# A list scheduler in the kernel file sets the order of a fused attention and feed-forward kernel

## The chip, the cores and the metric

The kernel runs on one core of one Trainium2 chip. The metric is the device time of one execution in microseconds, and of several runs the median. Names of engines: PE (TensorE matmuls) with PEld (its weight loads), DVE (VectorE), ACT (ScalarE), POOL (GpSimd, here only issuing stores), SP (SyncE, issuing loads and the output's stores).

## What is computed

Channel attention over q, k, v of 4 x 6080 x 256, whose result of 24320 rows of 256 goes through a feed-forward layer of width 2048 with a squared ReLU:

```python
qn = q / (np.linalg.norm(q, axis=1, keepdims=True) + 1e-06)
kn = k / (np.linalg.norm(k, axis=1, keepdims=True) + 1e-06)
s = kn.transpose(0, 2, 1) @ qn / tau
s = s - s.max(-1, keepdims=True)
a = np.exp(s)
a /= a.sum(-1, keepdims=True) + 1e-09
x = v @ a
...
h = x @ w_in
r = np.maximum(h, 0.0)
g = r * r
return g @ w_out
```

The attention matrix a is only 256 x 256 for each of the 4 batches.

## The kernel before

**Precision.** Every f32 operand of a large matmul is split into a high half (a cast to fp32r) and a low half (f32 minus the high half, again fp32r), and a product is three matmuls: high by high, low by high, high by low. So each operand costs a cast (on ACT in the kernel before) and a subtraction (on DVE).

**Work per batch.** The scores k'q are summed over 48 tiles of 128 rows, two at a time (`score_load`, `score_norm`, `score_split`, `score_mm`, `score_add`). Batch 0, and the first 24 tiles of batch 1 (the early scores, EARLY = 12 pairs), go through plain f32 matmuls on x and on an output bank (L175), the rest through split ones. `norms`, `spread`, `exps` and `attnT` make the softmax and turn it round. `fold` multiplies w_in by the attention matrix (L294), so that v is multiplied by the folded weights alone; `combine` makes from them the seven weight combinations of a Strassen product, wt, which POOL stores to memory (wsc, L320) and SP loads again for each later chunk (`load_wt`, L333; three buffers).

**Work per quad.** A batch's 6080 rows are 6 chunks of 2 x 512 (the last 2 x 480) rows; for each chunk there are 8 tiles j of the hidden width, and a pair (chunk, j) is a quad: 192 in all. The first layer of a quad is seven products, `m1` to `m7`, of three matmuls each, all issued on L386 in `product`. Their banks in PSUM are h (two), x and z:

- `m1` writes h; ACT copies it to x (L437). `m6` adds to h; ACT copies that to z (L445). `m4` adds to h again.
- `m7` writes the other h; ACT copies it to the tile m (L460).
- `m2` adds to x; ACT takes its ReLU to r (L452). `m5` adds to z, and DVE adds m to z with a ReLU, into s (L465); only then may `m3` add to z again; ACT takes the ReLU of that to r (L487). DVE also adds m to the h of `m4` (L465).
- `pair` squares s or r on ACT (L397), casts it to the high half of g (L401; on DVE, L399, for the last three j of a chunk and r alone) and subtracts (DVE, L402).

The second layer (`layer2`, `layer2s`, `run_later`, all on L547 in `accumulate`) multiplies g by w_out into four output banks o and, in chunks 2 to 23, j = 0, 2 and 4, saves products by a second Strassen scheme (`combos`, `split_later`; tiles D and t).

**What sets the order.** The program emits steps in the order of a plan (per quad `m1, m7, 0, m6, m2, 1, m5, m4, 2, m3`, where the numbers stand for second-layer products of the quad before). Side work (scores, folds, loads, splits of v) is put at fractional places between quads with `at`; `tie` adds an ordering edge, so that an instruction of side work doesn't come earlier than AHEAD = 1.0 quads before its place on PE, ACT and DVE. The framework's scheduler then orders everything by priority; copies out of PSUM are raised:

```python
459         with tc.high_priority():
460             nc.scalar.copy(out=state[q]["m7"][:, :T], in_=H[:, :T])
```

At the start six matmuls on a tile of ones run while the first loads are under way:

```python
635     busy = h_bank()
636     for _ in range(6):
637         nc.tensor.matmul(out=busy[:, :P], lhsT=ones, rhs=ones, start=True, stop=True)
```

Each engine executes its own instructions strictly in the order in which they stand, waiting on semaphores of the others.

## Time and profile before

| | |
|---|---|
| median of 3 runs | 2157.55 us (2156.49 to 2157.71) |
| the profiled execution, its own time | 2155.96 us |
| span of its instructions | 2154.2 us, 27293 instructions |
| PE / PEld busy | 2133.3 us (99%) / 1757.4 us (82%) |
| DVE / ACT busy | 1648.3 us (77%) / 1657.7 us (77%) |
| POOL busy | 42.7 us (2%) |
| DMA | 452.55 MB, mean 210 GB/s |

The busy time of PE is the union of its matmuls' times. Matmuls are pipelined and their ends are modelled: the mean duration of one is 389 ns where they follow each other every 226 ns or so, and a matmul that waits a little for its weights shows no idle time. An f32 matmul on unsplit tiles appears as two passes. The execution's own time has 1.8 us more than the span of its instructions.

### The profile page before, as it was taken

Reading aid. Unit: us, or ns where it says so; the run is one execution under the profiler, and the core shown is the slowest. Engines: PE = TensorE matmul, PEld = TensorE weight load, DVE = VectorE, ACT = ScalarE, POOL = GpSimd, SP = SyncE. Lnnn points to the kernel's source line nnn. Section 1 sums busy time; section 2 is a strip of 40 time slices with the busy share of each in tenths; the row PEclk is TensorE's granted clock in tenths of the full one; section 3 lists DMA queues with packets and bytes.
Section 4 is the critical chain, followed back from the end, with each engine's and each line's share of the span. In section 5 each row is a group of like instructions: output and inputs, shape, how many; then the busy total and the mean of one; then the engine's idle time right before and its main releaser. Section 6 shows DMA issues by size and latency. Waiting matters only on the chain.

```text
span 2154.2 us, 27293 instructions
## 1 busy us (share of the span) xinstructions
PE 2133.3 (99%) x9710; PEld 1757.4 (82%) x9710; DVE 1648.3 (77%) x2336; ACT 1657.7 (77%) x2512; POOL 42.7 (2%) x69
## 2 busy tenths in 40 slices
PE   9999999999999999999999999999999999999999
PEld 8778888878888888887888888888788788787787
DVE  6887778868779888786787978878778667667666
ACT  6788787877878878788788788877877767767766
POOL 0111000000000000000000000000000000000000
PEclk9999999999999999999999999999999999999999
DMA  9758755457585574556667656555566555555552
GB/s 351 290 228 310 249 174 212 157 206 249 194 288 206 176 247 166 197 180 210 232 214 256 230 176 223 177 194 194 201 234 226 197 189 181 181 184 186 181 169 90
DMA packets 125224, 452.55 MB, mean 210 GB/s; under 512 B 12928, under 2 KB 33920, under 8 KB 125088
## 3 DMA queue, kind: packets, MB, share of 16 engines
q1 hardware_dynamic: 117792, 412.40, 55.3%
q0 software_dynamic: 7296, 38.41, 4.5%
q8 instruction: 77, 1.26, 0.2%
q14 instruction: 59, 0.48, 0.1%
HBM read 387.45 MB, written 63.31 MB: 209 GB/s over the span
## 4 chain that ended last, share of the span: by engine, by line
PE 87%; ACT 7%; DVE 5%; issue 1%; DMA 1%; SPq 0%; ACTq 0%; DVEq 0%
PE o L547 34%; PE h L386 21%; PE z L386 11%; PE h L547 8%; PE x L386 5%; PE h L175 4%; PE h L294 2%; PE x L175 2%; DVE g L402 1%; DVE s L465 1%; ACT s L397 1%; ACT r L397 1%; ACT g L401 1%; ACT m L460 1%; ACT r L487 1%
## 5 line engine op out<-in xcount | busy, mean ns | idle before, releaser
L547 PE MATMUL o<-g,wo 128*128 128x512 f32 (+1 forms) x3420 | 896.2, 389 | 0.6 <-ACT g L401 0.4
L547 PEld LDWEIGHTS o<-g,wo 128*128 128x128 f32 x3420 | 637.3, 188 | 137.4 <-DVE g L402 8.9
L386 PE MATMUL h<-vt,wt 128*128 128x512 f32 (+1 forms) x2304 | 630.7, 389 | 4.1 <-ACT m L460 2.9
L386 PEld LDWEIGHTS h<-vt,wt 128*128 128x128 f32 x2304 | 430.5, 188 | 98.7 <-ACT m L460 5.6
L386 PE MATMUL z<-vt,wt 128*128 128x512 f32 (+1 forms) x1152 | 332.9, 393 | 4.0 <-ACT z L445 2.6
L402 DVE TENSOR_TENSOR g<-s,g 128x1024 fp32r<-128x1024 f32 (+1 forms) x126 | 152.8, 1213 | 174.4 <-ACT g L401 174.3
L402 DVE TENSOR_TENSOR g<-r,g 128x1024 fp32r<-128x1024 f32 (+1 forms) x192 | 232.5, 1211 | 52.3 <-ACT g L401 49.9
L386 PEld LDWEIGHTS z<-vt,wt 128*128 128x128 f32 x1152 | 209.2, 188 | 55.8 <-DVE s L465 12.5
L397 ACT ACTIVATE s<-s 128x1024 f32<-128x1024 f32 (+1 forms) x126 | 132.7, 1053 | 134.3 <-DVE s L465 134.0
L397 ACT ACTIVATE r<-r 128x1024 f32<-128x1024 f32 (+1 forms) x192 | 202.7, 1056 | 1.1
L386 PE MATMUL x<-vt,wt 128*128 128x512 f32 (+1 forms) x576 | 161.7, 387 | 0.0
L437 ACT COPY x<-h 128x512 f32<-128x512 f32 (+1 forms) x192 | 111.0, 578 | 49.3 <-PE h L386 47.4
L422 ACT ACTIVATE D<-D 128x1024 f32<-128x1024 f32 (+1 forms) x66 | 69.4, 1052 | 98.7 <-DVE D L465 98.4
L487 ACT ACTIVATE r<-z 128x512 f32<-128x512 f32 (+1 forms) x192 | 112.3, 585 | 42.8 <-PE z L386 41.7
L401 ACT CAST g<-s 128x1024 fp32r<-128x1024 f32 (+1 forms) x126 | 131.6, 1045 | 0.7
L386 PEld LDWEIGHTS x<-vt,wt 128*128 128x128 f32 x576 | 108.1, 188 | 21.8
L401 ACT CAST g<-r 128x1024 fp32r<-128x1024 f32 (+1 forms) x120 | 124.9, 1040 | 0.0
L155 DVE TENSOR_TENSOR acc<-acc,sq 128x1024 f32<-128x1024 f32 x92 | 112.1, 1219 | 11.8 <-ACT sq L154 9.4
L452 ACT ACTIVATE r<-x 128x512 f32<-128x512 f32 (+1 forms) x192 | 114.2, 595 | 4.2 <-DVE g L402 1.7
L445 ACT COPY z<-h 128x512 f32<-128x512 f32 (+1 forms) x192 | 112.6, 587 | 5.6 <-PE h L386 4.8
L460 ACT COPY m<-h 128x512 f32<-128x512 f32 (+1 forms) x192 | 111.6, 581 | 4.8 <-PE h L386 4.2
L373 DVE TENSOR_TENSOR vt<-v,vt 128x512 fp32r<-128x512 f32 (+1 forms) x144 | 94.2, 681 | 25.8 <-ACT vt L372 25.8
(154 smaller groups left out, 2726.1 us busy)
## 6 DMA issues: line engine op xcount, KB each, us to landing
wt<-wsc SPq DMA_DIRECT2D x184, 896.0 KB, 4.9
wo<-wop SPq DMA_DIRECT2D x118, 512.0 KB, 3.6
kq<-kq SPq DMA_DIRECT2D x87, 512.0 KB, 5.3
wo<-wodM SPq DMA_DIRECT2D x88, 384.0 KB, 4.2
wsc<-wt POOLq DMA_DIRECT2D x32, 896.0 KB, 5.8
wo<-wos SPq DMA_DIRECT2D x66, 384.0 KB, 3.6
v<-vT SPq DMA_DIRECT2D x40, 512.0 KB, 7.1
outT<-uM SPq DMA_DIRECT2D x80, 256.0 KB, 3.4
```

Source lines behind the costliest of these rows:

```text
L155: nc.vector.tensor_add(out=accs[b], in0=accs[b], in1=sq)
L175: nc.tensor.matmul(out=s[:, h * C:(h + 1) * C], lhsT=l, rhs=r, start=first and h == 0 and n == 0, stop=last and n == len(terms) - 1, skip_ ...
L386: nc.tensor.matmul(out=out[:, :T], lhsT=w[:, l, i], rhs=v[:, r, :T], start=start and n == 0, stop=n == 2, skip_group_check=True)
L397: nc.scalar.activation(out=x, in_=x, func=AF.Square)
L401: nc.scalar.copy(out=h, in_=x)
L402: nc.vector.tensor_sub(out=l, in0=x, in1=h)
L437: nc.scalar.copy(out=st["X"][:, :T], in_=st["B"][:, :T])
L445: nc.scalar.copy(out=st["Z"][:, :T], in_=st["B"][:, :T])
L452: nc.scalar.activation(out=state[q]["r"][:, 0, :T], in_=state[q]["X"][:, :T], func=AF.Relu)
L460: nc.scalar.copy(out=state[q]["m7"][:, :T], in_=H[:, :T])
L487: nc.scalar.activation(out=r[:, 1, :T], in_=state[q]["Z"][:, :T], func=AF.Relu)
L547: nc.tensor.matmul(out=o[:, :T], lhsT=l, rhs=r[:, :T], start=start and k == 0, stop=stop and k == 2)
```

## The change

The whole body is rewritten into two steps. First every operation is recorded with `add`: a key (its place in quads, as `at` had it), the engines that may do it with a cost for each, the tiles that it reads and writes, and a function that emits it. Then `Plan.order` runs a list scheduler over all operations, from front to back in its own time: for each of PE, ACT, DVE, SP and POOL it takes, whenever that engine is free, one of the operations whose inputs are ready and whose buffers are free. PE, SP and POOL take the one with the lowest key within a window (0.7 quads for PE); ACT and DVE take the one whose result is due first, counted back from PE's order, where DVE treats an operation that either engine could do as due 3.0 us later. The costs are lines in the number of columns (`vec`, `vec1`, `act`, `mm3`) and fixed latencies. What comes out is emitted with the framework's own ordering switched off (`tc.manual_schedule()`); the framework still places the semaphores and buffers.

Casts to fp32r (`split`) may now go to either engine; the copies out of PSUM (`moved`) stay on ACT, sums and subtractions on DVE. The products, their number and their tiling, the number of loads and stores and the sizes of the buffers stay. The six matmuls on ones are gone. Of the 24 early score tiles of batch 1, the last six (from LEAD = 18 on) get keys within the first quad. On PE the new program has 9534 matmul instructions where the old has 9540; on DVE there are 408 casts to fp32r where there were 72, on ACT 332 instructions fewer.

```diff
+    LAT = {"P": 0.22, "A": 0.16, "V": 0.14}
...
+    def __init__(self, rings, ahead, loose):
+        self.rings = rings
+        self.loose = loose
+        self.shy = {"V": 3.0}
+        self.ahead = ahead
...
+    def add(self, key, engines, fn, r=(), w=(), size=0):
...
+            if t in self.writer:
+                op.deps.add(self.writer[t])
...
+    def order(self):
...
+                    for op in waiting[e]:
+                        if op.ready > now + 1e-9 or op.key > place + self.ahead[e]:
+                            continue
+                        rank = (op.key, op.n) if e in "PSG" else (
+                            op.due + self.shy.get(e, 0.0) * (len(op.engines) > 1), op.n)
+                        if best is not None and rank >= best[0]:
+                            continue
+                        need = {}
+                        for name in op.tiles:
+                            if name not in live:
+                                need.setdefault(self.ring_of[name], []).append(turn[name])
+                        if any(free[ring] < len(n) or ring not in self.loose and max(n) >= served[ring] + len(n)
+                               for ring, n in need.items()):
+                            continue
+                        best = rank, op
+                    if best is None:
+                        continue
...
+                    op.begun = now
+                    out.append((op, e))
+                    at[e] = now + op.engines[e]
+                    done = at[e] + self.LAT.get(e, 0.0)
...
+def vec(n):
+    return 0.07 + 0.00104 * n
+
+
+def vec1(n):
+    return 0.07 + 0.00052 * n
+
+
+def act(n):
+    return 0.1 + 0.00083 * n
...
+    LEAD = 18
...
+    RINGS = {"kq": 4, "g2": 3, "D": 3, "hl": 2, "t4": 1, "s": 2, "sq": 2, "wo": 6, "wt": 3, "vt": 8, "v": 1, "tt": 1,
+             "m7": 2, "uM1": 1, "uM5": 1, "uM6": 1, "uM7": 1, "acc": 1, "s_acc": 1, "zq": 1, "e": 2, "den": 2,
+             "aT": 1, "y": 3, "nm": 2,
+             "h": 2, "x": 1, "z": 1, "o00": 1, "o01": 1, "o10": 1, "o11": 1}
+    plan = Plan(RINGS, {"P": 0.7, "A": 1.2, "V": 1.2, "S": 2.0, "G": 2.0}, ("h",))
...
+    def cast(n):
+        return {"A": act(n), "V": vec1(n)}
+
+    def alu(key, n, fn, r, w):
+        add(key, {"V": vec(n)}, lambda e: fn(), r, w)
+
+    def split(key, n, x, h, l, r, wh, wl):
+        add(key, cast(n), lambda e: copy(e, h(), x()), r, wh)
+        add(key, {"V": vec(n)}, lambda e: nc.vector.tensor_sub(out=l(), in0=x(), in1=h()), (*r, *wh), wl)
...
-    def pair(q, x, cs):
-        T = chunks[q[0]][2]
-        hl = work.tile([P, 2, 2, HMAX], F32R, name="g2", tag="g2", bufs=GB)
-        h, l = hl[:, 0, :, :T], hl[:, 1, :, :T]
-        nc.scalar.activation(out=x, in_=x, func=AF.Square)
-        if cs[0] == "11" and q[1] >= NJ - 3:
-            nc.vector.tensor_copy(out=h, in_=x)
-        else:
-            nc.scalar.copy(out=h, in_=x)
...
+    def pair(key, q, s, cs, view):
+        T = chunks[q[0]][2]
+        g = plan.tile("g2", ("g", q, cs))
+        add(key, {"A": act(2 * T)}, lambda e: square(e, view(), view()), [(s, 0), (s, 1)],
+            [(s, 0), (s, 1)])
+        split(key, 2 * T, view, lambda: get(g, [P, 2, 2, HMAX], F32R)[:, 0, :, :T],
+              lambda: get(g, [P, 2, 2, HMAX], F32R)[:, 1, :, :T], [(s, 0), (s, 1)], [(g, 0)], [(g, 1)])
...
-    def m7(q):
-        T = chunks[q[0]][2]
-        H = h_bank()
-        product(q, S3, H, True)
-        state[q]["m7"] = work.tile([P, HMAX], F32, name="m7")
-        with tc.high_priority():
-            nc.scalar.copy(out=state[q]["m7"][:, :T], in_=H[:, :T])
...
+    def m7(key, q):
+        T = chunks[q[0]][2]
+        H, m = plan.tile("h", ("H", q)), plan.tile("m7", ("m7", q))
+        product(key, q, S3, H, True)
+        add(key, moved(T), lambda e: copy(e, get(m, [P, HMAX])[:, :T], made[H][:, :T]), [(H, 0)], [(m, 0)])
...
-    busy = h_bank()
-    for _ in range(6):
-        nc.tensor.matmul(out=busy[:, :P], lhsT=ones, rhs=ones, start=True, stop=True)
...
+            at(-0.6 + 0.01 * k if k < LEAD else 0.02 + 0.9 * (k - LEAD) / (2 * EARLY - LEAD),
+               lambda key, g=g, t=t, k=k: score_mm(key, tiles0[1, g], t, s1, k == 0, k == EARLY * G - 1))
...
-    def tie(u, fn, args):
-        behind = next((last for t, last in reversed(marks) if t <= u - AHEAD), {})
-        n0 = len(traced())
-        fn(*args)
-        for ins in traced()[n0:]:
-            if ins.engine in behind:
-                tc.add_manual_dep(ins, behind[ins.engine],
-                                  mybir.DependencyInfo(mybir.DependencyClass.NoSync, mybir.DependencyReason.DATA),
-                                  reason="side work keeps its place")
...
+    for u, _, fn, args in sorted(events, key=lambda x: x[:2]):
+        fn(u, *args)
+    with tc.manual_schedule():
+        for op, e in plan.order():
+            op.fn(e)
```

Three places, each before and now. Ahead of a row's number of repetitions stand the tiles (out<-in) and the size.

PE from the end of the first pair of folds to the first second-layer products. L175 (L418 in the changed file) are the early scores on an output bank, L294 (L552) the folds, L386 (L661) the seven products, L547 (L805) the second layer. Before:

```order
L294 MATMUL h<-hl,aTl 128x512
L175 MATMUL o_369<-kq 128x256 x12
L175 MATMUL o_369<-g_337 128x256 x4
L175 MATMUL o_369<-g_367 128x256 x4
L175 MATMUL o_369<-D 128x256 x12
L386 MATMUL h<-vt,wt 128x512 x9
L386 MATMUL x<-vt,wt 128x512 x3
L386 MATMUL z<-vt,wt 128x512 x3
L386 MATMUL h<-vt,wt 128x512 x3
L386 MATMUL z<-vt,wt 128x512 x3
L294 MATMUL h<-hl,aTh 128x512
L386 MATMUL h<-vt,wt 128x512 x3
```

Now:

```order
L418 MATMUL o_362<-kq 128x256 x10
L418 MATMUL o_362<-g_282 128x256 x4
L418 MATMUL o_362<-g_372 128x256 x2
L661 MATMUL h<-vt,wt 128x512 x3
L418 MATMUL o_362<-g_372 128x256 x2
L661 MATMUL h<-vt,wt 128x512 x3
L418 MATMUL o_362<-D 128x256 x2
L661 MATMUL h<-vt,wt 128x512 x3
L418 MATMUL o_362<-D 128x256 x2
L661 MATMUL x<-vt,wt 128x512 x3
L418 MATMUL o_362<-D 128x256 x2
L552 MATMUL h<-hl,aT 128x512 x6
```

The 32 early score matmuls stood in one piece ahead of the first product; now 14 of them stand in twos between the products and the second fold.

ACT in quad 36. The copies into x, m7 and z are those behind `m1`, `m7` and `m6`; L397 (L273) squares s or r, L487 (L279) is the ReLU out of z, L269 is every copy and cast of the changed file. Before:

```order
L426 CAST t4_3966<-r_3906 128x512
L437 COPY x_4046<-h_4042 128x512
L397 ACTIVATE s_4009<-s_4009 128x1024
L487 ACTIVATE r_3997<-z_3992 128x512
L460 COPY m7_4054<-h_4050 128x512
L445 COPY z_4067<-h_4042 128x512
L401 CAST g2_4015<-s_4009 128x1024
```

Now:

```order
L269 CAST t4_4010<-s_3908 128x512
L269 COPY x_4029<-h_4020 128x512
L273 ACTIVATE s_4031<-s_4031 128x1024
L279 ACTIVATE s_3993<-z_3988 128x512
L269 CAST wt_4060<-kq_3830 128x256
L269 COPY z_4062<-h_4020 128x512
L269 COPY m7_4065<-h_4050 128x512
L273 ACTIVATE s_3993<-s_3993 128x1024
```

The square and the ReLU out of z still stand ahead of the two copies; a cast for wt has come between, and the copies have changed places.

DVE at the same place. L465 (L699) are the two sums that take z and h out of PSUM, L402 and L427 (L294) subtractions, L359 (L631, L639) combinations of v. Before:

```order
L427 TENSOR_TENSOR t4_3966<-r_3906,t4_3966 128x512
L359 TENSOR_TENSOR tt_4048<-v_3885 128x480
L465 ISA s_4009<-z_3992,m7_3979 128x512
L465 ISA s_4009<-h_3969,m7_3979 128x512
L280 TENSOR_TENSOR hl_4080<-kq_4002,hl_4080 128x1024
L465 ISA D_4090<-z_4067,m7_4054 128x512
L402 TENSOR_TENSOR g2_4015<-s_4009,g2_4015 128x1024
L465 ISA D_4090<-h_4042,m7_4054 128x512
```

Now:

```order
L294 TENSOR_TENSOR t4_4010<-s_3908,t4_4010 128x512
L639 TENSOR_TENSOR v_3706<-v_3706 128x480
L699 ISA s_4031<-z_3988,m7_3985 128x512
L699 ISA s_4031<-h_3944,m7_3985 128x512
L269 CAST hl_4046<-D_3757 128x512
L269 CAST hl_4046<-D_3931 128x512
L294 TENSOR_TENSOR hl_4046<-D_3757,hl_4046 128x512
L269 CAST g2_4055<-s_4031 128x1024
L294 TENSOR_TENSOR hl_4046<-D_3931,hl_4046 128x512
L294 TENSOR_TENSOR g2_4055<-s_4031,g2_4055 128x1024
```

A combination of v has moved in ahead of the first sum, and behind the sums stand three casts that were ACT's.

## Rows read from the trace of the kernel before

**Rows 1.** The page, part 1: busy us, share, instructions by engine.

```profile
PE 2133.3 (99%) x9710; PEld 1757.4 (82%) x9710; DVE 1648.3 (77%) x2336; ACT 1657.7 (77%) x2512; POOL 42.7 (2%) x69
```

**Rows 2.** Windows, two dense stretches: length, busy us (instructions), clock, DMA share, GB/s.

```profile
10.00:44.00 34.00, 34.00 (x159) 29.94 (x158) 28.37 (x25) 22.90 (x22) 0.00 (x0) 1.00 0.98 368
1722.00:1764.00 42.00, 42.00 (x186) 34.60 (x185) 30.89 (x44) 28.35 (x44) 0.00 (x0) 1.00 0.59 201
```

**Rows 3.** Windows, whole span, of lines L547, L386, L294, L175 in turn.

```profile
0.00:2155.00 2155.00, 1111.17 (x4410) 821.19 (x4410) 1.00 0.60 210
0.00:2155.00 2155.00, 1025.88 (x4032) 747.50 (x4032) 1.00 0.60 210
0.00:2155.00 2155.00, 51.61 (x192) 35.31 (x192) 1.00 0.60 210
0.00:2155.00 2155.00, 163.72 (x1008) 151.64 (x1008) 1.00 0.60 210
```

**Rows 4.** Windows of the start, the first quads, the rest.

```profile
0.00:49.00 49.00, 45.34 (x212) 39.91 (x212) 30.45 (x34) 28.84 (x30) 0.84 (x7) 1.00 0.93 346
49.00:130.00 81.00, 75.51 (x326) 59.40 (x324) 67.19 (x109) 63.33 (x107) 8.73 (x15) 1.00 0.71 266
130.00:2150.00 2020.00, 2012.37 (x9175) 1658.08 (x9174) 1549.89 (x2194) 1565.50 (x2377) 33.16 (x47) 1.00 0.59 205
```

**Rows 5.** Timeline, PE, at both ends: start us, us, instructions [idle us <-releaser].

```profile
1.14 2.93 PE L637 MATMUL h<-ones 128*128 128x128 f32 x12 [1.14 <-POOL ones L58]
...
3.86 1.98 PE L175 MATMUL x<-kq 128*128 128x256 f32 x8
...
8.36 3.94 PE L175 MATMUL x<-kq 128*128 128x256 f32 x17 [2.52 <-DMA kq<-kq]
...
52.80 0.60 PE L255 MATMUL h<-ident,e 128*128 128x128 f32 x4
...
2142.10 7.96 PE L547 MATMUL o<-g,wo 128*128 128x480 f32 x36
```

**Rows 6.** Timeline, PE, in the first quads.

```profile
81.25 0.96 PE L386 MATMUL z<-vt,wt 128*128 128x512 f32 x3 [0.45 <-DVE s L465]
84.35 0.50 PE L294 MATMUL h<-hl,aTh 128*128 128x512 f32 x1 [2.14 <-ACT hl L279]
```

**Rows 7.** Waits, weight loads, from 130 us on: us, times, longest.

```profile
PEld z L386 <- DVE s L465: 10.6, 40, 0.9
PEld o L547 <- DVE g L402: 8.2, 27, 0.6
PEld h L386 <- ACT m L460: 5.6, 6, 1.0
```

**Rows 8.** Timeline, ACT and then PE, around 470 us.

```profile
470.53 1.06 ACT L397 ACTIVATE s<-s 128x1024 f32<-128x1024 f32 x1 [1.46 <-DVE s L465]
471.50 0.58 ACT L487 ACTIVATE r<-z 128x512 f32<-128x512 f32 x1
471.97 0.58 ACT L460 COPY m<-h 128x512 f32<-128x512 f32 x1
472.44 0.60 ACT L445 COPY z<-h 128x512 f32<-128x512 f32 x1
...
473.09 0.96 PE L386 MATMUL z<-vt,wt 128*128 128x512 f32 x3 [0.40 <-ACT z L445]
```

**Rows 9.** Groups by line: count | busy us, mean ns | idle before.

```profile
L401 ACT CAST g<-s 128x1024 fp32r<-128x1024 f32 (+1 forms) x126 | 131.6, 1045 | 0.7
...
L426 ACT CAST kq<-D 128x512 fp32r<-128x512 f32 (+1 forms) x136 | 81.2, 619 | 5.4 <-PE h L547 5.1
...
L399 DVE CAST g<-r 128x1024 fp32r<-128x1024 f32 (+1 forms) x72 | 49.2, 683 | 7.9 <-ACT r L397 7.9
...
L81 DVE TENSOR_SCALAR hl<-kq 128x512 f32<-128x512 f32 x12 | 4.7, 421 | 0.1
```

**Rows 10.** Waits, SP's queue in the span, PE from 130 us on.

```profile
SPq L333 <- DMA wsc<-wt: 84.9, 24, 7.1
...
PE h L386 <- DMA wt<-wsc: 0.6, 2, 0.4
```

More of the change, by code (lines that the diff above doesn't have):

```diff
@@ L91, in tile_channel_attention_relu2_ffn, with store @@
+    def store(key, out, in_, r, w, size, e="G"):
+        add(key, {e: 0.45 if e == "S" else 1.0},
+            lambda e: (nc.sync if e == "S" else nc.gpsimd).dma_start(out=out(), in_=in_()), r, w, size)
+    win = {}
     wiv = w_in.bitcast(U32).rearrange("(h p) (t f) -> p h t f", p=P, t=2)
     wov = w_out.bitcast(U32).rearrange("(t g j p) e -> p g t j e", p=P, t=2, j=2)
-    win = {}
-    def load_f64(key, views):
-        tag, n = ("kq", KB) if key[1] else ("vt", VB)
-        parts = raws[key] = [work.tile([P, 2, GW, 2], U32, name=tag, tag=tag, bufs=n) for _ in range(2)]
-        for part, view in zip(parts, views):
-            nc.sync.dma_start(out=part.rearrange("p j n two -> p j (n two)"), in_=view)
@@ L123, in decode_w_out, with decode_w_in, wo_parts @@
+    def decode_w_in(key, g, lead=0.9):
+        Wn = decode(key, "in", g, "sq" if g else "t4", lead)
+        win[0, g] = Wn
+        store(key, lambda: dtile(("wins", g), [P, 4, GW]), lambda: made[Wn], [(Wn, 0)], [(("wins", g), 0)], 512)
+    def wo_parts(t):
+        return [t[:, k].rearrange("p (f e) c -> p f (e c)", f=2) for k in range(2)]
+    def decode_w_out(key, g, lead=0.9):
+        Wn = decode(key, "out", g, "sq", lead)
         for i in range(2):
             j = 2 * g + i
-            t = wo[0, j] = work.tile([P, 2, 4, P], F32R, name="wo", tag="wo", bufs=OB)
@@ new lines, in spread @@
+    def spread(key, b):
+        diag, bank = ("diag", b), plan.tile("h", ("zb", b))
+        zq = plan.tile("zq", ("zqs", b))
+        tiny(key, "P", 0.45, lambda: nc.tensor.matmul(
+            out=get(bank, [P, HMAX])[:, :C], lhsT=ones, rhs=made[diag].rearrange("p d c -> p (d c)"),
+            start=True, stop=True), [(diag, 0)], [(bank, 0)])
+        add(key, {"A": act(256), "V": vec(256)}, lambda e: copy(e, get(zq, [P, NH, P]).rearrange("p d c -> p (d c)"),
+                                                               made[bank][:, :C]), [(bank, 0)], [(zq, 0)])
@@ L382, in product, with mm3, strassen @@
+    KS = [0 if ci < 2 else 3 for ci in range(len(chunks))]
+    def mm3(T):
+        return 3 * (0.0155 + T * 0.000413)
+    def strassen(q):
+        return q[1] in SJ[:KS[q[0]]]
+    def product(key, q, i, bank, start):
         ci, j = q
         T = chunks[ci][2]
[L384 to L387 removed]
@@ new lines, in run, with m1 @@
+        def run(e):
+            out = get(bank, [P, HMAX])
+            for n, (l, r) in enumerate(((0, 0), (0, 1), (1, 0))):
+                nc.tensor.matmul(out=out[:, :T], lhsT=made[w][:, l, i], rhs=made[v][:, r, :T],
+                                 start=start and n == 0, stop=n == 2, skip_group_check=True)
+        add(key, {"P": mm3(T)}, run, [(v, 0), (v, 1), *wt_tokens(ci, j), *(() if start else [(bank, 0)])], [(bank, 0)])
+    def m1(key, q):
+        T = chunks[q[0]][2]
+        Bn, X = plan.tile("h", ("B", q)), plan.tile("x", ("X", q))
+        product(key, q, A11, Bn, True)
+        add(key, moved(T), lambda e: copy(e, get(X, [P, HMAX])[:, :T], made[Bn][:, :T]), [(Bn, 0)], [(X, 0)])
@@ new lines, in accumulate, with run, hl_of @@
+    def accumulate(key, bank, T, w, g, start, stop, r):
+        def run(e):
+            (wh, wl), (gh, gl) = w(), g()
+            o = get(bank, [P, HMAX])
+            for k, (l, x) in enumerate(((wh, gh), (wl, gh), (wh, gl))):
+                nc.tensor.matmul(out=o[:, :T], lhsT=l, rhs=x[:, :T], start=start and k == 0, stop=stop and k == 2)
+        add(key, {"P": mm3(T)}, run, [*r, *(() if start else [(bank, 0)])], [(bank, 0)])
+    def hl_of(ci, m, k):
+        return ("kl", ci, m, k) if k > 1 or ci >= (B - 1) * NCH else ("lh", ci, m)
```

1154 lines of the change are left out of this document (625 added, 529 removed).

## Prediction

> **What bounds the kernel now.** I read the page's busy line first, then a comparison of PE's densest stretches with the whole, then the two ends, then the waits. On the page PE is busy 99% of the span, DVE 77%, ACT 77% [rows 1], so PE is the bound, and the first question is how much of PE's 2133.3 us is work and how much is waiting that pipelined matmuls hide. Two stretches in which PE never idles give the price of work: 42.00 us hold 186 matmuls of 480 or 512 columns, 0.2258 us each, and 34.00 us hold 159 passes of the plain f32 scores, 0.214 us each [rows 2]. The reader should see in the counts that 4410 + 4032 + 192 = 8634 matmuls are of the first kind, and that the 1008 of L175 are 288 passes over whole f32 tiles and 720 of 256 columns over split ones [rows 3]. For the 720 no clean stretch exists; half of 0.2258, 0.113, is the least they can cost. The sum is 8634 x 0.2258 + 288 x 0.214 + 720 x 0.113 = 1949.5 + 61.6 + 81.4 = 2092.5 us. The span is 2154.2, so at most 61.7 us is not dense work.
>
> Of these, 3.9 us pass before the first score matmul, 2.5 us is the wait for the second load, and 4.1 us follow the last matmul (2142.10 + 7.96 = 2150.06) [rows 5]; the change touches none of them, as the loads and the last products stand in the same order. So some 51 us are open to a better order at the very most. From below: idle time that PE shows is 81 - 75.51 = 5.5 us in the first quads and 2020 - 2012.37 = 7.6 us from 130 us on [rows 4], together 13.1 us. The truth lies between 13 and 51. I take 40, nearer the upper end, since the three largest kinds of late weight loads alone come to 24.4 us [rows 7] where PE shows 7.6 us of idleness: most of the waiting is hidden. I put 9 of the 40 into the first quads and 31 into the rest.
>
> The Trainium skill (Perfetto Trace Analysis, Identifying the Most-Contended Engine) says to judge the distance to the limit by the weight loads' busy share and not by the matmuls'. By that the 82% of PEld [rows 1] would leave 18% of the span, 388 us, and a sum near 1770. The trace does not agree that this is room: in the dense stretch PEld is busy 34.60 of 42.00 us, also 82% [rows 2]. The measurement decides.
>
> **The change, part by part.**
>
> *The order of PE.* The matmuls are the same but for six that warm up. In the first quads the old order runs all remaining early scores ahead of the first product; the new one keeps 14 of 32 for the holes between products and folds (first pair of listings). Behind the products PE now waits 0.45 us for DVE's sum in z and 2.14 us for a cast of the folded weights [rows 6]; one early score is two passes, 0.43 us, so 14 of them cover 6.0 us. I take 6 of the 9 us. Bounds: 0, if the decode on ACT and DVE is late by as much again, and 9.
>
> *The rest of the span.* Three kinds of waits lead [rows 7]. For DVE's sum ahead of the last product into z (10.6 us): 58 of 192 quads have nine or fewer matmuls between the two products on z, and 33 in the new order, 43% fewer. For the low half of g (8.2 us) I found no such count, and nothing that makes it worse. For the copy of m7 (5.6 us), nothing is won where I looked: at 470 us ACT holds the copies of m7 and z behind a square that waits 1.46 us for DVE, and PE loses 0.40 us on z [rows 8]; in the new order the same square stands ahead of the same copies, with one more cast between (second pair). So I let 13 of the 31 us go, 42%, the share of the first kind. Bounds: 0 and 31.
>
> *The warm-up.* The six matmuls on ones are gone. They are 12 passes of 128 columns in 2.93 us, 0.24 each, as much as a pass of 256 columns later (3.94 / 17 = 0.23); a pass of 128 columns at 52.80 us takes 0.60 / 4 = 0.15 with its tail [rows 5]. So by the durations PE starts at the lower of its two levels, 1.2 GHz, and is at 2.4 GHz by 3.9 us, after 2.7 us of those matmuls (the granted clock of 1.00 over the whole stretch [rows 4] does not resolve this). Without them PE first works at about 3.9 us. The first load's eight passes become slower by 8 x 0.23 = 1.8 us, which the 2.52 us wait for the second load hides. Then PE stands still, and the stretch after 8.36 us has no idle time to hide anything. If 2.7 us of it run at the lower level again, it loses half of that, 1.4 us. Bounds: 0 (risen by then) and 2.7 (twice as long). I take +1.4.
>
> *The casts.* DVE has 408 casts in place of 72; 336 left ACT, 101 of 960 or 1024 columns, 215 of 480 or 512 and 20 smaller. On DVE a wide one is 683 ns; a 512 one has no row of its own, the nearest is 421 ns for a DVE operation on 512 f32, between half of the wide one, 341, and all of it [rows 9]. I take 421. With 0.4 us as an upper bound for the small ones on either engine, DVE gains 101 x 0.683 + 215 x 0.421 + 20 x 0.4 = 167 us, to about 1816 us (84%). ACT loses 101 x 1.045 + 215 x 0.619 + 20 x 0.4 = 247 us, to about 1411 (66%). Neither is the bound, so on PE's path I cost this at nothing; the cover is DVE's remaining 16%, and the first rival says what happens where it is gone. Late next on the path are then DVE's sums from PSUM.
>
> *The queues.* SP has the same loads; w_in and v of the first quads swap places with one score tile. POOL's stores of the two kinds of weights alternate differently. I take 0; SP's waits for a store are in the third rival.
>
> Sum, against the profiled execution's own 2155.96 us: 2155.96 - 6 - 13 + 1.4 = 2138.4, rounded to **2138 us**. The median of the three runs, 2157.55, is 1.6 above that execution; the runs differ by 1.2 among themselves, so I don't add it. 0.2% (4.3 us) is about what a measurement of this kernel can tell from no change.
>
> **The rivals.**
>
> *DVE becomes late (slower).* The sum that frees z stands on DVE, and the third pair of listings shows two casts right behind it and a subtraction of v ahead of it, which the old order has elsewhere. In the first quads DVE is already busy 67.19 of 81 us [rows 4]; 167 us more, unevenly spread, pass 95% in places. Price: if in a quarter of the 192 quads one cast of 0.683 comes ahead of a sum with no cover left, 48 x 0.683 = 33 us, and no gain but the first quads': 2155.96 - 6 + 1.4 + 33 = 2184; with half of that, **2168**. It decides where DVE's share in a stretch exceeds some 95%. Against it: the shares are 77% and 84%, and casts go to DVE when the scheduler sees ACT taken. Chance 0.14.
>
> *The waits move (no change).* The new order wins what I count and loses as much at other places, since the dependencies and buffers are the same: 2155.96 + 1.4, **2157**. For it: at the one late place examined nothing improves. Chance 0.13.
>
> *Stores wait for DVE (no change).* SP's queue waited 24 times, 84.9 us in all, for a store of wt on POOL to land before it could refill that buffer; PE then waited 0.6 us for such loads, twice [rows 10]. If each of the 24 stores is late by one wide cast and nothing covers it, 24 x 0.683 = 16.4 us: 2138 + 16 = **2154**. The Trainium skill (SBUF — State Buffer, Who interferes with whom) has such a rule: a DVE instruction in a two-port mode shuts GpSimd out of the shared ports, so descriptors for POOL's transfers come later. No row here isolates it; 72 such casts ran beside 0.6 us of PE's waits. Chance 0.03.
>
> *All of it goes (faster still).* The casts off ACT let its copies come on time too, and PE runs dense: 2155.96 - 40 + 1.4 = **2117**. Chance 0.10.
>
> That the framework reorders after all is no case: the built order has the new casts in new places.
>
> **How the numbers follow.** My forecast has 0.60; its own range, 6 to 31 us of gain with the clock's bounds, is 2125 to 2151. Faster by over 0.2% (below 2153.2) holds the forecast and the last rival, 0.70; no change 0.13 + 0.03 = 0.16; slower 0.14. The range 2119 to 2163 leaves out most of the slow rival (0.13) and the best of the fast one (0.05).
>
> **What would show it.** Right: PE's idle time in the stretch from 49 to 130 us falls from 5.5 to about 2 us; the same windows from 130 us on show more matmuls per us; the passes after the second load take 0.43 us instead of 0.22 for some 3 us; DVE near 84%, ACT near 66%. The forecast is wrong if waits for DVE's sums grow, if loads of wt end PE's waits more than a few times, or if the first quads' idle time stays.

## The result, and the profile after

The changed kernel takes **2134.27 us** (median of 5 runs, 2132.30 to 2134.49) where the kernel before takes 2156.49 us beside it (5 runs, 2155.07 to 2157.71): 22.2 us less, ratio 0.9895 with a 95% interval of 0.988 to 0.9909. The forecast was 2138 in a range of 2119 to 2163. The sign and the range held; the time is 4 us below the forecast, and the gain comes mostly from one of the three terms, as the rows below show. The profiled execution is the one of 2132.30 us: TensorE's mean granted clock was 1.000 in it and in the one of 2132.76 us, and 0.999 in the three of 2134.27 to 2134.49 us.

The busy lines of the page, which answer to [rows 1]:

```profile
span 2130.5 us, 27009 instructions
PE 2111.4 (99%) x9698; PEld 1765.8 (83%) x9698; DVE 1790.6 (84%) x2668; ACT 1469.4 (69%) x2180; POOL 39.2 (2%) x69
```

PE still reads 99%: this number could not show the gain, before or after. The windows can. They answer to [rows 4] (length, busy us and instructions of PE, PEld, DVE, ACT, POOL, clock, DMA share, GB/s), but the last one is 2000 us long here:

```profile
49.00:130.00 81.00, 75.23 (x330) 60.42 (x328) 69.54 (x123) 55.68 (x94) 8.81 (x15) 1.00 0.73 276
130.00:2130.00 2000.00, 1991.01 (x9168) 1666.31 (x9168) 1684.79 (x2510) 1381.40 (x2053) 28.48 (x46) 1.00 0.58 206
```

The same 2000 us of the kernel before:

```profile
130.00:2130.00 2000.00, 1992.37 (x9085) 1641.31 (x9085) 1537.39 (x2177) 1557.75 (x2366) 33.16 (x47) 1.00 0.60 207
```

The reader should look at the counts and not at the busy time. PE is busy for 1.4 us *less* and does 83 matmuls more; at the dense price of 0.2258 us [rows 2] these are 18.7 us. In the first quads PE is idle for 81 - 75.23 = 5.8 us, where it was 5.5, and does 4 matmuls more (330 against 326). The cut at 130 us matters here: in the changed kernel one wait of 1.7 us ends at 129.99 us, just inside. Up to 140 us, before and then after:

```profile
49.00:140.00 91.00, 84.42 (x361) 65.77 (x360) 77.16 (x123) 70.62 (x117) 9.27 (x16) 1.00 0.69 262
49.00:140.00 91.00, 85.23 (x373) 68.63 (x372) 78.99 (x140) 63.40 (x108) 8.81 (x15) 1.00 0.66 250
```

Here PE is idle for 5.8 us against 6.6 and does 12 matmuls more, 2.7 us of dense work. So the first quads won some 1 to 3 us, by where the cut stands, and not the 6 of the forecast.

The waits of the weight loads from 130 us on (total us, times, longest), against [rows 7]:

```profile
PEld z L661 <- ACT z L269: 9.9, 11, 1.5
PEld z L661 <- DVE s L699: 2.1, 1, 2.1
PEld h L418 <- ACT m L269: 0.9, 2, 0.5
PEld o L805 <- DVE t L294: 0.8, 2, 0.4
PEld h L661 <- ACT x L269: 0.5, 3, 0.2
```

All three kinds that led before are nearly gone: for DVE's sum from 10.6 us in 40 waits to a single one of 2.1 us (it is the one that ends at 129.99 us, so it began in the first quads), for the low half of g from 8.2 to no row, for m7's copy ahead of products from 5.6 to no row. One kind has grown. In the kernel before it was the fourth:

```profile
PEld z L386 <- ACT z L445: 5.1, 7, 0.8
```

So `m5`, which adds to z, now waits for ACT's copy into z, and this is most of what is left.

**A measure for the experiments.** I took the time from each matmul's start to the next, less the dense price for its size (227 ns for 512 columns, 216 for 480 and for a pass of plain f32, 118 for 256, 109 to 214 for the small ones), and added up what is over; where a record starts early, its shortfall is carried to the next. The sum is called *stall*. It includes the wait for the second load and slow passes at the start, and a wait is counted where it begins. Before, it is 12.7 us in the first 130 us and 39.4 in the rest, 52.1 in all; after, 11.1 and 17.9, 29.0 in all. The difference, 23.1, meets that of the two spans, 2154.2 - 2130.5 = 23.7. Span less stall is 2102.1 before and 2101.5 after: the work itself has not changed, and the prediction's 2092.5 us of dense work with 8 us at the two ends, 2100.5, was right to 2 us.

### The profile page after: what moved, and what is told of

Same layout as the page of the kernel before. It is cut to its first block, busy times and chain, and to the rows that moved or that the text cites. A ratio compares the mean times of both kernels' runs of the same rounds, so it can differ in the third digit from the quotient of the medians.

```text
span 2130.5 us, 27009 instructions
## 1 busy us (share of the span) xinstructions
PE 2111.4 (99%) x9698; PEld 1765.8 (83%) x9698; DVE 1790.6 (84%) x2668; ACT 1469.4 (69%) x2180; POOL 39.2 (2%) x69
## 4 chain that ended last, share of the span: by engine, by line
PE 88%; DVE 6%; issue 2%; ACT 2%; DMA 1%; SPq 0%; ACTq 0%; DVEq 0%; POOLq 0%
PE o L805 35%; PE h L661 22%; PE z L661 11%; PE h L805 8%; PE x L661 5%; PE h L418 4%; PE h L552 2%; PE x L418 1%; DVE g L294 1%; DVE s L699 1%; DVE hl L294 1%; ACT s L273 1%; DVE wt L294 0%; DMA vt<-w_in 0%; DMA D<-kq 0%
## 5 line engine op out<-in xcount | busy, mean ns | idle before, releaser
L805 PE MATMUL o<-g,wo 128*128 128x512 f32 (+1 forms) x3420 | 883.6, 388 | 0.5 <-DVE g L294 0.5
L805 PEld LDWEIGHTS o<-g,wo 128*128 128x128 f32 x3420 | 636.9, 188 | 124.5 <-DVE g L294 1.1
L661 PE MATMUL h<-vt,wt 128*128 128x512 f32 (+1 forms) x2304 | 623.4, 388 | 0.0
L661 PEld LDWEIGHTS h<-vt,wt 128*128 128x128 f32 x2304 | 430.9, 188 | 88.2 <-ACT x L269 0.5
L273 ACT ACTIVATE s<-s 128x1024 f32<-128x1024 f32 (+1 forms) x318 | 335.3, 1054 | 140.8 <-DVE s L699 140.4
L294 DVE TENSOR_TENSOR g<-s,g 128x1024 fp32r<-128x1024 f32 (+1 forms) x318 | 384.8, 1210 | 49.1 <-ACT g L269 45.7
L661 PE MATMUL z<-vt,wt 128*128 128x512 f32 (+1 forms) x1152 | 324.6, 390 | 8.0 <-ACT z L269 6.0
L661 PEld LDWEIGHTS z<-vt,wt 128*128 128x128 f32 x1152 | 212.4, 188 | 53.5 <-ACT z L269 11.7
L269 ACT CAST g<-s 128x1024 fp32r<-128x1024 f32 (+1 forms) x158 | 164.9, 1044 | 1.8
L661 PE MATMUL x<-vt,wt 128*128 128x512 f32 (+1 forms) x576 | 161.0, 388 | 0.0
L279 ACT ACTIVATE s<-z 128x512 f32<-128x512 f32 (+1 forms) x192 | 112.7, 587 | 66.9 <-PE z L661 65.9
L269 ACT COPY x<-h 128x512 f32<-128x512 f32 (+1 forms) x192 | 110.2, 574 | 70.5 <-PE h L661 65.4
L273 ACT ACTIVATE D<-D 128x1024 f32<-128x1024 f32 (+1 forms) x66 | 69.3, 1051 | 120.6 <-DVE D L699 120.6
L269 DVE CAST g<-s 128x1024 fp32r<-128x1024 f32 (+1 forms) x160 | 109.7, 686 | 31.5 <-ACT s L273 31.4
L661 PEld LDWEIGHTS x<-vt,wt 128*128 128x128 f32 x576 | 108.1, 188 | 21.6
L269 ACT COPY z<-h 128x512 f32<-128x512 f32 (+1 forms) x192 | 111.9, 583 | 17.6 <-PE h L661 16.9
L279 ACT ACTIVATE s<-x 128x512 f32<-128x512 f32 (+1 forms) x192 | 114.1, 594 | 5.1 <-PE x L661 0.7
L805 PE MATMUL h<-kq,wo 128*128 128x512 f32 (+1 forms) x408 | 114.4, 389 | 0.0
L269 ACT COPY m<-h 128x512 f32<-128x512 f32 (+1 forms) x192 | 110.5, 576 | 1.8 <-PE h L661 0.8
L418 PEld LDWEIGHTS h<-hl 128*128 128x128 f32 x720 | 101.4, 189 | 10.4 <-ACT m L269 0.9
L805 PE MATMUL h<-hl,wo 128*128 128x512 f32 (+1 forms) x384 | 107.2, 387 | 0.0
```

The source lines that it names most:

```text
L269: (nc.scalar.copy if e == "A" else nc.vector.tensor_copy)(out=out, in_=in_)
L273: nc.scalar.activation(out=out, in_=in_, func=AF.Square)
L279: nc.scalar.activation(out=out, in_=in_, func=AF.Relu)
L294: add(key, {"V": vec(n)}, lambda e: nc.vector.tensor_sub(out=l(), in0=x(), in1=h()), (*r, *wh), wl)
L418: nc.tensor.matmul(out=s[:, h * C:(h + 1) * C], lhsT=l, rhs=r, start=first and h == 0 and n == 0, stop=last and n == len(terms) - 1, skip_ ...
L661: nc.tensor.matmul(out=out[:, :T], lhsT=made[w][:, l, i], rhs=made[v][:, r, :T], start=start and n == 0, stop=n == 2, skip_group_check=True)
```

## The experiments

Twelve kernels ran, each beside the kernel before (2156.98 to 2157.24 us in these comparisons). Stall is that of the one profiled execution.

| kernel | median us | ratio to before, 95% interval | stall to 130 us | stall after |
|---|---|---|---|---|
| before | | | 12.7 | 39.4 |
| casts_as_before | 2156.35 | 0.9998 (0.9989 to 1.0007) | 13.9 | 37.9 |
| before_casts_dve | 2152.25 | 0.9978 (0.9969 to 0.9987) | 14.3 | 36.5 |
| casts_by_rule | 2163.21 | 1.0030 (1.0018 to 1.0042) | 15.4 | 45.0 |
| after | 2134.27 | 0.9895 (0.9880 to 0.9909) | 11.1 | 17.9 |
| act_dve_by_key | 2146.65 | 0.9952 (0.9937 to 0.9967) | 11.2 | 28.5 |
| flat_costs | 2184.48 | 1.0125 (1.0110 to 1.0140) | 14.0 | 63.5 |
| pe_in_key_order | 2265.59 | 1.0500 (1.0483 to 1.0518) | 36.0 | 126.1 |
| no_shy | 2136.57 | 0.9907 (0.9891 to 0.9924) | 12.6 | 21.1 |
| early_in_one_piece | 2135.86 | 0.9900 (0.9884 to 0.9917) | 12.7 | 21.0 |
| warm_up_back | 2134.72 | 0.9898 (0.9883 to 0.9913) | 13.0 | 18.4 |
| hold_for_urgent | 2126.45 | 0.9861 (0.9846 to 0.9875) | 12.9 | 11.7 |
| hold_and_reach | 2125.24 | 0.9853 (0.9838 to 0.9867) | 10.6 | 9.7 |
| casts_before_hold | 2154.51 | 0.9989 (0.9980 to 0.9999) | 13.7 | 37.0 |

### Is it the order, or the casts?

**casts_as_before**: the list scheduler, but with each cast on the engine that it had.

```diff
-    def cast(n):
-        return {"A": act(n), "V": vec1(n)}
+    def cast(n, on):
+        return {"A": act(n)} if on == "A" else {"V": vec1(n)}
```

(`split` passes "V" for `pair`'s casts of r with `q[1] >= NJ - 3`, else "A"; the copy in `spread` is ACT's.)

> The new list scheduler, but each cast stays on the engine that it had before (72 on DVE, all others on ACT). Theory A, the order does it: copies and sums come on time because the scheduler knows their durations, and the casts only follow along; then nearly all of the 22.2 us stay won, 2134 to 2140 us, with ACT near 77% and DVE near 77% busy as before. Theory B, the room on ACT does it: ACT's copies of z and m7 come late because casts and squares of 1.05 us stand ahead of them, and only 336 casts fewer change that; then most of the gain goes, 2150 to 2157 us, and PE waits for ACT's copies (m7, z) again by 10 us or more. Theory C, order and free choice work only together: 2150 to 2170 us, PE's waits for ACT longer than in the kernel before.

Measured: 2156.35 us, 0.9 below the kernel before, which cannot be told from no gain. The waits of its weight loads from 130 us on:

```profile
PEld z L661 <- ACT z L269: 30.4, 29, 1.8
PEld h L661 <- ACT x L269: 4.0, 11, 0.5
PEld o L806 <- DVE g L294: 3.1, 9, 1.0
```

The three kinds of [rows 7] have shrunk here too, the waits for DVE's sum to no row among these. But the wait for z's copy, 5.1 us in the kernel before, is 30.4. The new order alone moves the waiting from DVE to one copy on ACT.

**before_casts_dve**: the framework's scheduler, and 348 casts on DVE by a fixed rule (the text on record says about 400).

```diff
-        if cs[0] == "11" and q[1] >= NJ - 3:
+        if q[1] in ((1, 3, 5, 6, 7) if cs[0] == "11" else (6, 7)):
...
-        nc.scalar.copy(out=t[:, 0, :T], in_=x)
+        (nc.vector.tensor_copy if i in (S2, S3) else nc.scalar.copy)(out=t[:, 0, :T], in_=x)
```

(`split_later` likewise for the second of its three tiles, and for the third in M6 and M7.)

> The framework's scheduler as before, but about 400 of the casts on DVE by a fixed rule (five of eight quads for one pair, two of eight for the other, three of the later products' seven splits, two of seven of v). Theory A, the order does it: no gain, 2150 to 2160 us. Theory B, the room on ACT does it: at least half of the 22.2 us, 2134 to 2146 us, with PE's waits for the copy of m7 (5.6 us before) nearly gone. Theory C, they work only together: no gain or a loss, 2153 to 2175 us, PE's waits for DVE's sums ahead of the last product into z above the 10.6 us of before.

Measured: 2152.25 us, 5.0 below the kernel before. ACT falls from 77% to 69% busy as in the changed kernel, and yet the same kinds of waits stand there, about as long as before:

```profile
PEld z L386 <- DVE s L465: 8.9, 36, 0.5
PEld o L547 <- DVE g L402: 6.2, 20, 0.4
PEld z L386 <- ACT z L445: 5.7, 10, 0.8
PEld h L547 <- ACT m L460: 5.0, 13, 0.5
PEld h L175 <- ACT m L460: 4.7, 9, 0.8
```

So one half of the change gives 0.9 us, the other 5.0, and both together 22.2: theory C, though neither half loses as that theory had it.

**casts_by_rule** joins both halves in another way: the list scheduler with the fixed rule of before_casts_dve, given to `split` as in casts_as_before.

> The new list scheduler with the casts of the run before_casts_dve: each on the engine that a fixed rule names, 348 of them on DVE. If it is the amount of work off ACT together with the new order (ACT 69% busy, as in the changed kernel), nearly all of the gain is there: 2134 to 2141 us. If it is the free choice in the moment, so that a cast goes to whichever engine is free and no copy of z waits behind it, the fixed rule loses most of it: 2148 to 2165 us, with PE waiting for ACT's copy of z by 15 us or more (9.9 us of weight loads in the changed kernel, 30.4 us with the casts of before).

Measured: 2163.21 us, slower than the kernel before, with ACT as free as in the changed kernel (busy line of the page):

```profile
PE 2122.6 (98%) x9698; PEld 1763.9 (82%) x9698; DVE 1771.8 (82%) x2608; ACT 1487.9 (69%) x2240; POOL 37.8 (2%) x69
```

Its longest wait of the weight loads from 130 us on:

```profile
PEld z L662 <- ACT z L269: 35.4, 32, 1.9
```

This was the run that decided. It isn't the amount of work taken off ACT (69% here and there), and it isn't the order alone: what is left is the choice, cast by cast, of the engine when the scheduler comes to it. Two things differ besides: the rule puts 348 casts on DVE and not 408, and a cast that is fixed on DVE has no delay of 3.0 us behind DVE's own work. The delay is not what makes the loss: the run no_shy below, without it, is 2.3 us above the changed kernel. Whether some other fixed rule, fitted to the times of the copies, could do as well was not tried.

### What the scheduler's three ingredients are worth

**pe_in_key_order**

```diff
-    plan = Plan(RINGS, {"P": 0.7, "A": 1.2, "V": 1.2, "S": 2.0, "G": 2.0}, ("h",))
+    plan = Plan(RINGS, {"P": 0.0, "A": 1.2, "V": 1.2, "S": 2.0, "G": 2.0}, ("h",))
```

> The scheduler may not take a PE step ahead of its key: PE's steps stand strictly in the order of the keys (the allowance of 0.7 quads is 0), ACT and DVE still choose by due time and casts still go to either engine. If timely copies and sums on ACT and DVE are the whole of it: no loss, 2134 to 2140 us. If PE is full because it fills each hole with whatever is ready: the holes between the two products into z and ahead of the second layer open again; each of 192 quads then has at least one exposed latency of 0.2 to 0.5 us, so 40 to 100 us more, 2175 to 2235 us.

Measured: 2265.59 us, 131 above the changed kernel and more than expected. PE's own idle time now shows which hole it had filled:

```profile
PE z L661 <- DVE s L699: 51.4, 35, 2.5
PE h L805 <- ACT m L269: 24.7, 20, 1.5
```

The sum in z ahead of `m3` leads. What closes that hole is work of other steps put between the two products on z, as the prediction had it from the order: here 111 of the 192 quads have nine or fewer matmuls between them, in the changed kernel 33. Not all of the 131 us is waiting: the mean granted clock is 0.992 here, with 0.50 from 52.9 to 69.8 us, where PE is busy for 8.0 of 16.9 us. An upper estimate of the clock's part is 0.008 x 2263.8 = 18 us.

**act_dve_by_key**

```diff
-                        rank = (op.key, op.n) if e in "PSG" else (
-                            op.due + self.shy.get(e, 0.0) * (len(op.engines) > 1), op.n)
+                        rank = (op.key, op.n)
```

> ACT and DVE take the ready work with the lowest key (its place in the program) instead of that with the earliest due time; costs, the engines open to casts and PE's freedom as in the changed kernel. If the due times bring copies and sums ahead of squares and casts, PE waits for them again: 2144 to 2157 us. If the key does as well, since work of the same quad comes in that order anyway: within 3 us of the changed kernel, 2131 to 2137 us.

Measured: 2146.65 us: without due times 12.4 of the 22 us go, and waits for m7's copy are back:

```profile
PEld h L660 <- ACT m L268: 5.6, 4, 1.9
PEld h L417 <- ACT m L268: 5.0, 5, 1.2
```

**flat_costs**: `vec`, `vec1` and `act` all return 0.65.

> The changed kernel with one cost, 0.65 us, for every ACT and DVE operation in the scheduler, whatever its size, in place of the durations by size (0.5 to 1.1 us); rules and freedoms as they were. If the order needs durations that hold on the chip: the order that the scheduler makes fits less well, PE waits for ACT and DVE again, and a third to all of the 22 us goes: 2142 to 2165 us. If the rules (due time, either engine, PE's reach) do it, and the waits on the chip set the pace anyway: 2131 to 2138 us.

Measured: 2184.48 us, 50 above the changed kernel and 27 above the one before, worse than either theory said. Nothing but the numbers given to the scheduler differs (with them it puts 361 casts on DVE), and PE waits for everything a little:

```profile
PEld z L661 <- ACT z L269: 14.0, 24, 1.3
PEld z L661 <- DVE s L699: 12.0, 21, 1.6
PEld h L661 <- ACT x L269: 8.0, 23, 0.7
PEld h L661 <- DVE uM L852: 7.0, 11, 1.3
```

**no_shy**: `self.shy = {"V": 0.0}`.

> The changed kernel without the 3 us by which DVE puts casts behind its own work of the same due time, so that casts go to DVE more freely. If DVE was the engine short of time (84% busy), its sums come late and PE waits for them: 2138 to 2150 us, DVE above 86%. If ACT is still the one whose copies come late (9.9 us of weight loads waiting for the copy of z), casts on DVE as often as it is free help a little more: 2127 to 2133 us.

Measured: 2136.57 us, 2.3 above the changed kernel with overlapping intervals: no difference that can be told, and in neither theory's range. With 470 casts, DVE is 85% busy there (1818.9 us). That DVE is nearly short of time is not borne out.

### The two small terms

**warm_up_back**: in `tc.manual_schedule()`, ahead of everything, the six matmuls on ones.

> The changed kernel with the six warm-up matmuls on ones at its start again. The prediction's step (+1.4 us for their absence): about 1.4 us faster than the changed kernel, 2132.9 us, and full granted clock near 4 us instead of near 7.9 us. The rival: the passes at the lower clock lie in the wait for the second load, which landed at 7.66 us in the trace after, so nothing is won, and the first score matmul starts behind the warm-up (3.86 instead of 3.56 us): 2134.0 to 2135.0 us.

Measured: 2134.72 us, not to be told from the time without them; by the intervals a difference of 1.4 us could not be told either. The starts of PE without and with them, in the two profiled executions (timeline: start us, us, what, idle before):

```profile
3.56 3.78 PE L418 MATMUL x<-kq 128*128 128x256 f32 x8 [3.56 <-DMA kq<-kq]
7.66 5.54 PE L418 MATMUL x<-kq 128*128 128x256 f32 x24 [0.32 <-DMA kq<-kq]
```

```profile
3.85 2.92 PE L418 MATMUL x<-kq 128*128 128x256 f32 x8
7.96 4.37 PE L418 MATMUL x<-kq 128*128 128x256 f32 x19 [1.19 <-DMA kq<-kq]
```

Without the warm-up the first eight passes take 3.78 us, nearly twice the 1.98 of [rows 5], so they run at the lower level of the clock. But they end before the second load lands, and behind it 24 passes take 5.54 us, 0.231 each, against 4.37 / 19 = 0.230 with the warm-up: in these two executions the clock costs nothing behind the load.

That is not so in every execution. hold_for_urgent and early_in_one_piece (below) start with the same passes and no warm-up. Behind the second load PE reads in them:

```profile
7.97 6.32 PE L423 MATMUL x<-kq 128*128 128x256 f32 x20 [0.66 <-DMA kq<-kq]
8.57 5.72 PE L418 MATMUL x<-kq 128*128 128x256 f32 x17 [1.15 <-DMA kq<-kq]
```

At 0.231 us a pass these would be 4.6 and 3.9 us: 1.7 and 1.8 us are lost. The first seven or eight passes still start some 0.43 us apart, the lower level, just as the prediction's step had it. Of the eleven traces without warm-up four have seven or eight such passes behind the load (casts_by_rule and pe_in_key_order are the others), and of the three with it one has seven, before_casts_dve. So a loss of the forecast size is real in some executions, warm-up matmuls do not rule it out, and the medians cannot say what they are worth.

The clock also fell later. In the trace of warm_up_back PE waits 2.08 us in the chain of norms, up to 53.65 us, and goes on at the lower level; in that of the changed kernel it waits 1.98 us at the same place and does not. The windows, changed kernel first:

```profile
54.00:57.00 3.00, 3.00 (x16) 2.64 (x15) 2.93 (x7) 1.23 (x4) 0.00 (x0) 1.00 1.03 415
54.00:57.00 3.00, 3.00 (x8) 2.37 (x8) 2.93 (x8) 0.97 (x3) 0.00 (x0) 0.50 1.02 415
```

Twelve score passes that take 2.75 us in the one take 4.01 us in the other.

**early_in_one_piece**

```diff
-            at(-0.6 + 0.01 * k if k < LEAD else 0.02 + 0.9 * (k - LEAD) / (2 * EARLY - LEAD),
+            at(-0.6 + 0.01 * k if k < LEAD else -0.3,
```

> The last early scores are keyed ahead of the first product instead of being spread over the first quad; the rest as in the changed kernel. The prediction's step (14 early scores as filler cover 6 us of waiting in the first quads): 3 to 6 us slower than the changed kernel, 2137 to 2140 us. Rival: they cover little, since the holes that remain there come before any product, in the chain of norms, softmax and fold; then within 1.5 us, 2133 to 2136 us.

Measured: 2135.86 us, 1.6 above the changed kernel, within the scatter. The stall to 130 us is 12.7 against 11.1, but the filler is not what makes this difference. In this trace the second load landed 0.9 us later (8.57 against 7.66 us), the slow passes behind it cost 1.8 us, and the clock fell behind the chain of norms, where the twelve passes take 4.30 us in place of 2.75. Together that is some 4.2 us, and the two profiled executions differ by 4.1 (2136.43 and 2132.30). So no run shows that the filler is worth anything. PE's idle time in the first quads agrees. Before (49 to 130 us), and then after:

```profile
PE h L294 <- ACT hl L279: 2.1, 1, 2.1
PE z L294 <- ACT hl L279: 1.3, 1, 1.3
PE z L386 <- DVE s L465: 1.0, 2, 0.5
```

```profile
PE h L483 <- DVE zq L475: 2.0, 1, 2.0
PE z L661 <- DVE s L699: 1.7, 1, 1.7
PE z L661 <- ACT z L269: 0.9, 2, 0.7
```

The waits for the cast of the folded weights, one of them the 2.14 us of [rows 6], are gone. In their place PE waits 2.0 us in the chain of norms at 53.20 us (`spread`), before any product, and 1.7 us for a sum at 129.99 us. But without the filler it is the same: in early_in_one_piece, from 49 to 140 us, no wait for that cast stands either, and both new ones do:

```profile
PE z L661 <- DVE s L699: 1.9, 2, 1.7
PE h L483 <- DVE zq L475: 1.9, 1, 1.9
```

The waits for that cast are gone in casts_as_before too. So the rest of the new order closed the holes that I had looked at, and the filler did not; about the same time came back at two others.

### What is left, and a faster version

The longest remaining wait for z, in ACT's timeline and then PE's (start us, duration us):

```profile
611.96 1.06 ACT L273 ACTIVATE s<-s 128x1024 f32<-128x1024 f32 x1 [1.12 <-DVE s L699]
612.92 0.58 ACT L279 ACTIVATE s<-z 128x512 f32<-128x512 f32 x1
613.40 1.05 ACT L273 ACTIVATE sq<-kq 128x1024 f32<-128x1024 f32 x1
614.35 0.59 ACT L269 COPY z<-h 128x512 f32<-128x512 f32 x1
```

```profile
613.09 0.84 PE L661 MATMUL x<-vt,wt 128*128 128x512 f32 x3
614.99 0.96 PE L661 MATMUL z<-vt,wt 128*128 128x512 f32 x3 [1.05 <-ACT z L269]
```

PE went on to x at 613.09 us, so the h that the copy reads was about to be complete; but at 613.40 ACT began a square for the norms, which DVE took up only at 614.92, and the copy started 0.95 us after it. The same four rows return at 1139.57 us; at 724.27 it is a cast of g that stands there; at 550 us the copy comes late in another way, behind a square that had waited for DVE. **hold_for_urgent** forbids the first two:

```diff
                     op = best[1]
+                    if e in "AV":
+                        lag = max(0.0, now - (pe[head].due if head < len(pe) else now))
+                        done = now + op.engines[e]
+                        if any(now + 1e-9 < u.ready < done - 0.4 and u.due + lag < done and u.due < op.due for u in waiting[e]):
+                            continue
```

> One rule added to the changed kernel's scheduler: ACT or DVE doesn't start a piece of work if something with an earlier due time becomes ready more than 0.4 us before that piece would end and is late by then. Theory: what is left of PE's waiting (8.3 us from start to start ahead of products into z, for ACT's copy of z) comes from a square or wide cast of 1.05 us begun just ahead of that copy; then 5 to 10 us go: 2124 to 2129 us. Rival: ACT's idle time brings other work late, and the waits move: 2132 to 2140 us.

Measured: 2126.45 us, 7.8 below the changed kernel; the intervals (0.9846 to 0.9875 and 0.988 to 0.9909) do not meet. Its longest wait from 130 us on, in sum:

```profile
PEld z L666 <- ACT z L274: 3.0, 6, 0.7
```

**hold_and_reach** adds freedom:

```diff
-    LEAD = 18
+    LEAD = 4
...
-    plan = Plan(RINGS, {"P": 0.7, "A": 1.2, "V": 1.2, "S": 2.0, "G": 2.0}, ("h",))
+    plan = Plan(RINGS, {"P": 1.1, "A": 2.0, "V": 2.0, "S": 2.0, "G": 2.0}, ("h",))
```

> The rule of the run hold_for_urgent, and more freedom: PE may take work up to 1.1 quads ahead of the key in place of 0.7, ACT and DVE up to 2.0 in place of 1.2, and 20 early scores in place of 6 are spread over the first quad. Theory: PE's remaining stalls (4.7 us from 130 us on in hold_for_urgent, and 14.3 us before) are holes that ready work further ahead can fill: 4 to 9 us below hold_for_urgent, 2117 to 2123 us, close to the end that the prediction gave for all waits gone. Rival: what remains are lone latencies of chains that no other work covers (norms, softmax, fold) and the small change of clock at the start; then 2124 to 2128 us.

Measured: 2125.24 us, the fastest, but in the rival's range and not to be told from hold_for_urgent. Its stall is 20.3 us; on z one wait of 1.1 us is left:

```profile
PEld z L666 <- ACT z L274: 1.1, 1, 1.1
```

Does holding do alone what the freedom of engine does? **casts_before_hold** is casts_as_before with the rule added.

> The casts fixed on the engines of before, as in casts_as_before (2156.35 us), with the rule of hold_for_urgent added. If the fixed casts cost only because the scheduler starts a long piece just ahead of an urgent copy, the rule gives back most of the 22 us without any freedom of engine: 2128 to 2138 us. If the freedom of engine does more than that (the rule lets ACT idle, and what it has to do, 77% of the span, comes late elsewhere), no more than the 8 us that the rule gave with free casts: 2146 to 2156 us.

Measured: 2154.51 us, 1.8 below casts_as_before, where the rule took 7.8 off the changed kernel. The wait for z's copy is shorter each time and comes oftener:

```profile
PEld z L666 <- ACT z L274: 26.0, 41, 1.2
PEld h L666 <- ACT x L274: 5.8, 10, 1.5
```

So a square begun too early is not all that delays the copy where casts have one engine only.

The Trainium skill (Perfetto Trace Analysis, Optimizing Scalar/DVE Operations) advises breaking up instructions of an engine that isn't saturated but causes bubbles on another. The 1.05 us square at 613.40 is such an instruction on an engine that is 69% busy; here the order did it, and a split square was not tried.

## Why the prediction was right, and where it was not

- **The bound.** Right: dense work of 2092.5 us and "some 51 us open" stand against 52.1 us of measured stall, which includes the wait for the second load. That 40 of them were waiting was too low; most of the rest was waiting too. The forecast's own range, 2125 to 2151, does not follow from the bounds of its terms: 40 us less and 2.7 us more give 2116 to 2159.
- **Order of PE, first quads, -6 us.** This step failed. Stall there went from 12.7 to 11.1 us, and idle time to 130 us rose from 5.5 to 5.8 instead of falling to 2; with the cut at 140 us some 3 us were won at the most. The prediction named this itself as a sign of being wrong: that the first quads' idle time stays. The step took the holes to be closed by the 14 early scores; early_in_one_piece shows them closed without these, and the step left out what is late in the new order in their place: the chain of norms and a sum at 130 us.
- **The rest of the span, -13 us.** The mechanism is right, the size is not: stall fell from 39.4 to 17.9, so the term measured about -21.5. I let 42% of the waiting go, the share that I had counted for DVE's sum. That wait fell from 10.6 us to the single one of 2.1 at the cut. I had put nothing on the low half of g and on m7's copy, where I had seen no reason or looked at one quad; these fell from 8.2 and 5.6 us to no row. Against this stands the growth of the wait for z's copy from 5.1 to 9.9, which only the rival "the waits move" had in it.
- **The warm-up, +1.4 us.** Nothing in the profiled execution, and open for the median. The slow passes were there, as said (3.78 us), and hidden, as said. That the clock would be at the lower level behind the second load was not so in this trace (0.231 us a pass), but was so in those of hold_for_urgent and early_in_one_piece, which lost 1.7 and 1.8 us there. The mechanism is right; that it takes part in only some executions was not in the step, and neither was the fall of the clock behind the chain of norms.
- **The casts, 0.** Wrong in what I made of it, though PE pays nothing for them on DVE. I counted the casts as an even load. Without the freedom of engine the gain is 0.9 us (casts_as_before). DVE came out at 1790.6 us for a forecast of 1816, ACT at 1469.4 for 1411. For a cast that stands close behind its neighbour, the whole duration is too much to add or take away: at 613.40 the square lasts 1.05 us, and the next instruction starts after 0.95. This explains a part of both differences; the rest is open.
- **The rivals.** *DVE becomes late*: DVE at 84% as forecast, but PE's wait for its sums fell, and no_shy, with more on DVE, lost nothing that can be told. *Stores wait for DVE*: SP's waits for the stores of wt went from 84.9 us in 24 [rows 10] to

```profile
SPq L297 <- DMA wsc<-wt: 79.6, 15, 10.4
```

  with no wait of PE for wt among its rows. *The waits move*: this is what the order does without free casts. *All of it goes*, 2117: hold_and_reach came to 2125.24.

Sum as measured from the traces: 2155.96 - 1.6 - 21.5 = 2132.9, with 0.3 us for the earlier first score 2132.6, against 2132.30 of the profiled execution. That it closes says only that the work stayed the same. The forecast's terms were off by 4.4 us one way and by 8.5 and 1.4 us the other, so a part of its nearness, 4 us, is luck.

## What to carry to other kernels

Where an engine reads 99% busy, count its instructions per window against a dense stretch: that gave the size of PE's waiting to 2 us, of which the fastest version won 31. A static order has to be judged together with the freedom of where work may run, since each half alone gave 0.9 and 5.0 us and both 22.2; and a list scheduler is as good as its durations (one flat cost made it 50 us worse) and must not start a long piece just ahead of an urgent short one. When you price a filled hole, look for the wait that comes next, and run the kernel without the filler before you credit it.

## What was not expected of the hardware

The same start does not run at the same clock each time. After eight plain f32 score passes in 3.78 us and 0.32 us of idleness PE stood at its higher level from 7.66 us on (0.231 us a pass); after the same eight and 0.66 us of idleness, in the trace of hold_for_urgent, it stayed at the lower one for seven passes more (20 in 6.32 us). Behind a wait of some 2 us near 53 us the granted clock was 1.00 in one trace and 0.50 in another, which made twelve passes 4.01 us long in place of 2.75. So a wait of PE can cost more than its own length, and a term of 1 to 2 us at the start can't be judged by one trace. And the second load landed at 7.66, 7.96, 8.36 and 8.57 us in four traces, which moves PE's start by as much as the terms that I had argued over there.
